# The first block's first layer for the last 768 tokens by Strassen's seven products, with weights combined two batches ahead

## The chip, the cores and the metric

The kernel runs on one core of a Trainium2 chip. The metric is the device time of one execution in microseconds (us), lower is better. Of a core's engines the text names TensorE (PE; its weight loads are PEld), VectorE (DVE), ScalarE (ACT), GpSimd (POOL) and SyncE (SP), which issues the transfers (DMA) here. Line numbers up to the prediction are those of the kernel before.

## What is computed

Three steps in fp32: a block-causal attention (4 batches, 8 heads, 576 tokens of 64 values a head), then a first block of three matrices whose outputs are combined by a maximum, then a second block with four experts:

```python
def _moe_ref(x, w1, w2, w3, w_out):          # x: 2304 x 512, w1..w3: 512 x 768, w_out: 768 x 512
    h = np.maximum(np.maximum(x @ w1, x @ w2), x @ w3)
    return h @ w_out

def _moe2_ref(x, domain_probs, w1, w2):      # w1: 4 x 512 x 1024, w2: 4 x 1024 x 512
    p = domain_probs / (domain_probs.sum(-1, keepdims=True) + 1e-09)
    for e in range(E):
        h = np.maximum(x @ w1[e], 0.0)
        out += p[:, e:e + 1] * (h @ w2[e])
    return out
```

`reference` applies attention, `_moe_ref` and `_moe2_ref` one after the other. The change concerns `x @ w1`, `x @ w2`, `x @ w3` of `_moe_ref` for the last 768 of the 2304 tokens.

## The kernel before

**Precision.** Every matmul of the blocks is made of three: a number is split into a high part and a low part (`f32r` tiles ending in `h` and `l`), and `mm3` (L475, matmul at L480) adds high x high, high x low and low x high in one PSUM tile.

**Attention.** The 16 pairs of heads go one after the other (n = 4 b + d, batch b). A pair's scores (`st`, L181 to L202) are on PE, the row minima (L218) on DVE, the exponentials (L225) on ACT, the sums' reciprocals (L233, L234) on DVE, the division (L251) on POOL; PE transposes the probabilities (`tt`, L279), DVE and ACT copy them out of PSUM (L289), and PE multiplies them with the values (`pv`, L314). Each pair runs its stages beside those of the next one.

**The first block, `moe1(b)` (L505).** Tokens 0 to 511 of a batch (`MAIN`) are one run of 512 columns; the last 64 tokens of each batch (`REST`) are collected in `rest_x`, and all 256 of them are a second run with batch 3. For each of 18 weight tiles (6 blocks `ff` of the hidden width x 3 matrices) a run takes 12 matmuls, over 4 blocks of the inner width with three terms each. The first matrix's result is copied to `mt` or `mr` (L524), the maximum with the others taken by DVE (L526), and POOL splits the hidden values (L528, L529). Then 4 tiles of the output layer take 18 matmuls a run (copied out at L537). Batch 0 splits the weights itself (`Convert`) and stores them to DRAM (`held`); the later batches load them, 512 KB a tile (`moe_weight`, L468).

**What sets the order.** `moe1(b)` is a generator: a unit is up to four matmuls. `Filler.upto` (L540) advances it between the stages of the next batch's attention, in proportion to the pairs done and `LAG` = 9 units behind, so batch b's first block lies under batch b + 1's attention. Batch 3's has no attention to lie under: it runs alone, behind it. Beside it the second block is prepared, with the filler advanced by 8 units between pieces: `combine(0)` (L693) makes the seven sums of token blocks that Strassen's method needs, and `weights_in(0, n)` (L811) loads 512 KB of the second block's weights (`t`, L819), makes their four sums on DVE (`combos`, L790 to L793), splits them (`halves`, ACT L797, DVE L799) and stores 1792 KB (`ka`, L822). The second block already multiplies by Strassen's seven products with 384 columns (L844). SP has one queue of transfers in program order.

## Time and profile before

| | |
|---|---|
| time, median of 3 runs | 1219.99 us (1219.66 to 1220.39) |
| the profiled execution | 1219.63 us, span 1217.7 us |
| PE busy | 1190.4 us, 98% of the span |
| DVE, ACT, POOL busy | 833.7, 466.9, 295.6 us (68, 38, 24%) |
| moved by DMA | 290.67 MB, mean 239 GB/s |

The span is the recorded part of the execution. The page gives busy time by engine and by group of instructions; the chain of waits follows the work that ended last backwards; the windows give busy time by engine in a stretch, the clock that TensorE was granted (PEclk, 1.00 is full) and the share of the DMA engines' time.

### The profile page before, as it was taken

To read this page: it belongs to the slowest core of one execution; us is meant where nothing else is said; L and a number is where in the kernel's file an instruction comes from. 1 tells how busy PE (TensorE), PEld (TensorE's weight loads), DVE (VectorE), ACT (ScalarE), POOL (GpSimd) and SP (SyncE) were. 2 spreads that over 40 slices of the span, in tenths; PEclk is the share of its full clock that TensorE was granted. 3 is DMA by queue.
4 is the path that set the end of the run, shared out by engine and by line. 5 is a ranking of instruction groups with operands and counts; after the bars stand their busy time and mean duration, and the time that the engine had idled before them with its cause. 6 is when DMAs were issued, how large, how long until landed. Compare 5 with 4: busy or idle time off the path is not lost.

```text
span 1217.7 us, 18226 instructions
## 1 busy us (share of the span) xinstructions
PE 1190.4 (98%) x6941; PEld 1065.0 (87%) x6941; DVE 833.7 (68%) x1453; ACT 466.9 (38%) x974; POOL 295.6 (24%) x324
## 2 busy tenths in 40 slices
PE   7889999999999999999999999999999999999998
PEld 4567777778777888898999989999999999999998
DVE  4877874443445541778888895758697887587896
ACT  5976665454335111344434340232232213322222
POOL 2458853433421220433333340000000000000000
PEclk8999999999999999999999999999999999999999
DMA  5836765554423784878888865777887877676664
GB/s 205 274 130 221 247 213 173 164 150 146 139 87 106 272 293 136 302 272 317 319 297 311 303 207 198 282 284 279 344 309 297 322 295 277 233 272 234 250 214 176
DMA packets 82347, 290.67 MB, mean 239 GB/s; under 512 B 8716, under 2 KB 18004, under 8 KB 69204
## 3 DMA queue, kind: packets, MB, share of 16 engines
q1 hardware_dynamic: 82260, 289.51, 67.3%
q8 instruction: 55, 0.90, 0.3%
q14 instruction: 32, 0.26, 0.1%
HBM read 206.34 MB, written 83.14 MB: 238 GB/s over the span
## 4 chain that ended last, share of the span: by engine, by line
PE 80%; DVE 8%; DMA 5%; ACT 4%; issue 2%; POOL 1%; SPq 0%; DVEq 0%; ACTq 0%; POOLq 0%
PE m L844 23%; PE m L480 23%; PE o L1003 16%; PE pv L314 3%; PE tt L279 3%; PE st L181 3%; PE o L926 2%; PE o L930 2%; PE o L929 2%; PE m L1003 2%; DMA part<-in_e_w 2%; ACT p L225 1%; DMA t<-in_e_w 1%; PE st L202 1%; DMA w<-kb 1%
## 5 line engine op out<-in xcount | busy, mean ns | idle before, releaser
L844 PE MATMUL m<-t,w 128*128 128x384 f32 x1152 | 228.4, 336 | 0.0
L1003 PE MATMUL o<-hx,w 128*128 128x384 f32 x1176 | 226.1, 337 | 0.5 <-DMA w<-kb 0.4
L1003 PEld LDWEIGHTS o<-hx,w 128*128 128x128 f32 x1176 | 207.7, 188 | 1.1 <-PE m L844 0.7
L844 PEld LDWEIGHTS m<-t,w 128*128 128x128 f32 x1152 | 203.4, 188 | 2.7 <-DVE tmp L864 0.3
L844 PE MATMUL m<-b,w 128*128 128x384 f32 x864 | 175.5, 336 | 2.1 <-ACT tmp L869 2.1
L844 PEld LDWEIGHTS m<-b,w 128*128 128x128 f32 x864 | 153.1, 188 | 5.6 <-ACT tmp L869 2.4
L480 PE MATMUL m<-xh,wt 128*128 128x512 f32 x352 | 117.4, 396 | 0.0
L225 ACT ACTIVATE p<-st,mn 128x128 f32<-128x128 f32 (+2 forms) x144 | 78.6, 557 | 54.7 <-DVE mn L218 54.7
L864 DVE TENSOR_TENSOR tmp<-m,tmp 128x384 f32<-128x384 f32 x144 | 77.8, 549 | 21.0 <-PE m L844 18.5
L251 POOL TENSOR_SCALAR p<-p,sm 128x128 f32<-128x128 f32 (+4 forms) x108 | 72.0, 683 | 69.1 <-ACT high L119 34.0
L218 DVE TENSOR_REDUCE mn<-st 128x1 f32<-128x128 f32 (+2 forms) x144 | 67.9, 512 | 17.6 <-ACT p L225 9.9
L974 ACT CAST hx<-hq 128x768 fp32r<-128x768 f32 x49 | 40.7, 837 | 97.5 <-PE o L1003 74.2
L480 PEld LDWEIGHTS m<-xh,wt 128*128 128x128 f32 x352 | 65.6, 188 | 12.6 <-ACT arena L537 0.2
L926 PE MATMUL o<-w,hh 128*128 128x512 f32 x192 | 74.8, 392 | 0.5 <-ACT hh L904 0.5
L929 PE MATMUL o<-w,hh 128*128 128x512 f32 x192 | 74.8, 390 | 0.0
L930 PE MATMUL o<-w,hl 128*128 128x512 f32 x192 | 74.7, 391 | 0.0
L279 PE MATMUL tt<-ident,p 128*128 128x128 f32 x400 | 62.7, 286 | 11.2 <-ACT eh L289 6.9
L799 POOL TENSOR_TENSOR w<-part,w 128x512 fp32r<-128x512 f32 x32 | 49.5, 1568 | 92.9 <-ACT w L797 92.9
L279 PEld LDWEIGHTS tt<-ident,p 128*128 128x128 f32 x400 | 48.0, 146 | 25.1 <-ACT eh L289 8.3
L480 PE MATMUL m<-xl,wt 128*128 128x512 f32 x176 | 69.3, 394 | 0.0
L480 PE MATMUL m<-hh,wo 128*128 128x512 f32 x192 | 64.0, 400 | 0.9 <-ACT wo L94 0.9
L799 POOL TENSOR_TENSOR part<-mix,part 128x512 fp32r<-128x512 f32 x32 | 43.8, 1382 | 71.6 <-ACT part L797 65.8
(184 smaller groups left out, 2112.1 us busy)
## 6 DMA issues: line engine op xcount, KB each, us to landing
w<-kb SPq DMA_DIRECT2D x55, 1024.0 KB, 6.0
w<-ka SPq DMA_DIRECT2D x30, 1792.0 KB, 7.9
ka<-w SPq DMA_DIRECT2D x16, 1792.0 KB, 6.7
wt<-held SPq DMA_DIRECT2D x34, 512.0 KB, 4.1
kb<-part SPq DMA_DIRECT2D x16, 1024.0 KB, 6.9
kb<-w SPq DMA_DIRECT2D x16, 768.0 KB, 4.8
arena<-in_w SPq DMA_DIRECT2D x18, 512.0 KB, 4.7
wo<-held SPq DMA_DIRECT2D x12, 768.0 KB, 4.4
```

The lines of the kernel that those rows point to most:

```text
L218: least.append(nc.vector.tensor_reduce(mn[:, m:m + 1], x, axis=AX.X, op=ALU.min))
L225: exps.append(nc.scalar.activation(to, x, ACTF.Exp, bias=mn[:, m:m + 1], scale=-1.0, accum_out=sm[:, m:m + 1],))
L251: normal.append(nc.gpsimd.tensor_scalar(x, x, sm[:, c:c + 1], 1.0, op0=ALU.mult, op1=ALU.mult))
L279: nc.tensor.transpose(tt[:, c:c + P], pt[i][:, k0:k0 + P], ident)
L480: nc.tensor.matmul(out=out_, lhsT=w, rhs=x, start=m == 0, stop=m == n - 1)
L799: eng.tensor_tensor(w[:, a:b, 1], raw[:, a:b], f(w[:, a:b, 0]), op=ALU.subtract)
L844: ins = nc.tensor.matmul(out=m, lhsT=a, rhs=b, start=start and n == 0, stop=stop and n == 3 * KH - 1, skip_group_check=True,)
L864: nc.vector.tensor_tensor(t, x, y, op=ALU.add)
L926: ins = nc.tensor.matmul(out=o, lhsT=hh[:, ts], rhs=wh, start=i == 0, stop=False)
L929: nc.tensor.matmul(out=o, lhsT=hh[:, ts], rhs=wl, start=False, stop=False)
L930: nc.tensor.matmul(out=o, lhsT=hl[:, ts], rhs=wh, start=False, stop=i == G - 1)
L1003: nc.tensor.matmul(out=o, lhsT=a, rhs=b, start=start and m == 0, stop=stop and m == 2, skip_group_check=True,)
```

## The change

Batch 3's first layer and the 256 last tokens are joined to 768 tokens in two halves of 384: tokens 0 to 383 of batch 3, and tokens 384 to 511 of batch 3 with the 256 tokens of `rest_x`. For each matrix n and each two blocks `ff` (9 groups) the 2 x 2 blocks of the weights and of the inputs are multiplied by seven products instead of eight, each product 6 matmuls of 384 columns (`moe1_last`). Three PSUM tiles hold them; partial sums (`u`, `v`, `q1`) are taken out and added by DVE.

The sums of weight blocks that this needs (`t1`, `t2`, `t3`, `b22`) are made by `sums` while batches 1 (groups 0 to 3) and 2 (groups 4 to 8) have the weights in SBUF: DVE adds high and low parts of two tiles (2 x 512 columns), makes four sums (256), ACT casts 1024 columns, DVE subtracts, and 1 MB is stored to DRAM (`summed`); one scratch buffer in `arena` serves all groups. For this, batches 1 and 2 take the tiles of two blocks `ff` in turn. `moe1_last` loads a group's plain parts (`w0` 512 KB, `w1` 256 KB) and its sums (`w2`, 1024 KB, into the tiles `xh` and `xl` in turn).

`rest_x` is one fp32 tile without a low part, and batch 3's inputs are no longer split by `moe1_inputs`; `combine(*ends)` makes the seven sums of inputs behind the attention. The filler's distance in batch 3's attention is 2 x `LAG`. The splitting of batch 3's hidden values is on ACT and DVE instead of POOL. The second block's `weights_in(0, n)` are 14 units apart, and its own `combine` comes behind them.

```diff
+SHARE = 4
...
+    summed = [dram.tile([P, 2, 4, 2 * P], F32, name=f"summed{i}") for i in range(3 * NF // 2)]
...
-    rest_x = [mp.tile([P, KD, B * REST], F32R, name=f"rx{i}", tag=f"rx{i}") for i in range(2)]
+    CT, KH = 384, KD // 2
+    OVER = MAIN - CT
+    NGRP = 3 * NF // 2
+    rest_x = mp.tile([P, KD, OVER + B * REST], F32, name="rx", tag="rx")
...
+            o = OVER + b * REST
+            nc.scalar.copy(rest_x[:, d, o:o + REST], xf[:, MAIN:S])
+            if b == B - 1:
+                nc.scalar.copy(rest_x[:, d, 0:OVER], xf[:, CT:MAIN])
+                continue
+            nc.scalar.copy(xh[:, d], xf[:, 0:MAIN])
+            nc.vector.tensor_tensor(xl[:, d], xf[:, 0:MAIN], f(xh[:, d]), op=ALU.subtract)
...
+    def sums(g, w0, w1):
+        o = 2 * KD * S
+        high, raw = (arena[:, o + i * 8 * P:o + (i + 1) * 8 * P] for i in range(2))
+        for i, w in enumerate((w0, w1)):
+            x = [w[:, j].rearrange("p a f -> p (a f)") for j in range(2)]
+            nc.vector.tensor_tensor(raw[:, i * 4 * P:(i + 1) * 4 * P], f(x[0]), f(x[1]), op=ALU.add)
+        a11, a12, a21, a22 = (raw[:, i * 2 * P:(i + 1) * 2 * P] for i in range(4))
+        nc.vector.tensor_tensor(a22, a21, a22, op=ALU.add)
+        nc.vector.tensor_tensor(a21, a11, a21, op=ALU.subtract)
+        nc.vector.tensor_tensor(a11, a22, a11, op=ALU.subtract)
+        nc.vector.tensor_tensor(a12, a12, a11, op=ALU.subtract)
+        nc.scalar.copy(high.bitcast(F32R), raw)
+        nc.vector.tensor_tensor(raw.bitcast(F32R), raw, high, op=ALU.subtract)
+        nc.sync.dma_start(
+            out=summed[g].rearrange("p x s f -> p (x s f)"), in_=arena[:, o:o + 16 * P]
+        )
...
+        if b:
+            order = [(2 * j + i, n) for j in range(NF // 2) for n in range(3) for i in range(2)]
+        else:
+            order = [(ff, n) for ff in range(NF) for n in range(3)]
...
+            if b and ff % 2:
+                g = 3 * (ff // 2) + n
+                if (g >= SHARE) == (b > 1):
+                    sums(g, last[0], wt)
+            last[0] = wt
...
+    def moe1_last(xc):
+        b = B - 1
...
+                w0 = moe_weight(b, 6 * j + n, at)
+                w1 = moe_weight(b, 6 * j + 3 + n, at + 1, KH)
...
+                nc.sync.dma_start(
+                    out=f(w2).rearrange("p x s f -> p (x s f)"),
+                    in_=summed[3 * j + n].rearrange("p x s f -> p (x s f)"),
+                )
...
+                def product(i, name, start, stop):
+                    first = True
+                    for k in range(KH):
+                        for x, y in ((0, 0), (0, 1), (1, 0)):
+                            nc.tensor.matmul(
+                                out=ms[i], lhsT=side(name, x, k), rhs=xc[name][:, y, k], start=start and first,
+                                stop=stop and (k, x) == (KH - 1, 1), skip_group_check=True,
+                            )
+                            first = False
...
+                def close(key, i, x=None):
+                    if n == 0:
+                        tag = ("mt", "mr")[key[1]]
+                        t = mp.tile([P, (MAIN, CT)[key[1]]], F32, name=tag, tag=tag, bufs=2)[:, 0:CT]
+                        state[key] = t
+                        if x is None:
+                            nc.scalar.copy(t, ms[i])
+                        else:
+                            plus(t, ms[i], x)
+                    else:
+                        t = state[key]
+                        x = ms[i] if x is None else plus(x, ms[i], x)
+                        nc.vector.tensor_tensor(t, x, t, op=ALU.max)
...
+                    for h, l, x in to:
+                        nc.scalar.copy(h, x)
+                        nc.vector.tensor_tensor(l, x, f(h), op=ALU.subtract)
...
+                product(0, "b11", True, False)
+                q1 = temp()
+                nc.scalar.copy(q1, ms[0])
+                yield
+                product(1, "t2", True, False)
+                u = plus(temp(), ms[1], q1)
+                yield
+                product(2, "t1", True, False)
+                v = plus(temp(), ms[2], q1)
+                yield
+                product(0, "b21", False, True)
+                close((0, 0), 0)
+                yield
+                product(1, "t3", False, False)
+                close((1, 1), 1, v)
+                yield
+                product(2, "b22", False, True)
+                close((0, 1), 2, u)
+                yield
+                product(1, "t4", False, True)
+                close((1, 0), 1, q1)
...
-            filler.upto((at - 1) * UNITS - LAG)
+            filler.upto((at - 1) * UNITS - (LAG if b < B - 1 else 2 * LAG))
...
-    following = combine(0)
+    ends = [x for ds in (slice(0, KH), slice(KH, KD)) for x in (x2f[B - 1][:, ds, 0:CT], rest_x[:, ds])]
+    following = combine(*ends)
+    xc = next(following)
+    filler.work.append(moe1_last(xc))
+    for _ in following:
+        filler.upto(filler.done + 1)
+    for n in (2, 3):
+        filler.upto(filler.done + 14)
+        weights_in(0, n)
+    ready = []
+    for n in range(2):
+        filler.upto(filler.done + 14)
+        ready.append(weights_in(0, n))
+    filler.upto(filler.done + 8)
+    following = combine(*blocks(0))
     xc = next(following)
     for _ in following:
-
-        filler.upto(filler.done + 8)
-    weights_in(0, 2)
-    filler.upto(filler.done + 8)
-    weights_in(0, 3)
-    filler.upto(filler.done + 8)
-    ready = [weights_in(0, n) for n in range(2)]
+        filler.upto(filler.done + 4)
```

In the rows of order each line is an instruction or a few alike, with its line in its own kernel. PE at the end of attention, before: transposes of the last pair's probabilities (`tt<-ident,p_...`) and the filler's output layer of batch 2 (`m<-hh,wo`):

```order
L279 MATMUL tt<-ident,p_3903 128x128 x4
L279 MATMUL tt<-ident,p_3782 128x128
L279 MATMUL tt<-ident,p_3780 128x128
L279 MATMUL tt<-ident,p_3782 128x128 x2
L480 MATMUL m<-hl,wo 128x512
L480 MATMUL m<-hh,wo 128x512
L279 MATMUL tt<-ident,p_3911 128x128 x2
L480 MATMUL m<-hh,wo 128x512
L480 MATMUL m<-hl,wo 128x512
L480 MATMUL m<-hh,wo 128x512 x2
L480 MATMUL m<-hl,wo 128x512
L480 MATMUL m<-hh,wo 128x512 x2
```

And in the changed kernel, from the transposes of the last pair to its output product:

```order
L284 MATMUL tt<-ident,p_3889 128x128 x4
L284 MATMUL tt<-ident,p_3755 128x128
L284 MATMUL tt<-ident,p_3753 128x128
L284 MATMUL tt<-ident,p_3755 128x128 x2
L284 MATMUL tt<-ident,p_3897 128x128 x2
L284 MATMUL tt<-ident,p_3902 128x128 x5
L284 MATMUL tt<-ident,p_3891 128x128 x4
L284 MATMUL tt<-ident,p_3763 128x128
L284 MATMUL tt<-ident,p_3761 128x128
L284 MATMUL tt<-ident,p_3763 128x128 x2
L284 MATMUL tt<-ident,p_3899 128x128 x2
L319 MATMUL pv_4149<-eh,vraw 64x384 x2
```

The filler's matmuls (L480, now L487) that stood between the transposes stand behind the last product `pv`.

SP's queue in the middle of the last layer, before: the second block's stores `ka` and loads `t`, and the tiles of the first block (`wt`, `wo` from `held`):

```order
L822 DMA ka_3_4188<-w_4590 128x3584
L819 DMA t<-in_e_w 128x1024
L468 DMA wt<-held_89 128x2x512
L468 DMA wo<-held_90 128x2x512
L468 DMA wo<-held_91 128x2x512
L822 DMA ka_0_4185<-w_4643 128x3584
L819 DMA t<-in_e_w 128x1024
```

And in the changed kernel, where `xh` and `xl` receive the sums:

```order
L958 DMA ka_3_4215<-w_4515 128x3584
L955 DMA t<-in_e_w 128x1024
L603 DMA xh<-summed_103 128x2048
L473 DMA wt<-held_85 128x2x512
L473 DMA wt<-held_88 128x2x256
L603 DMA xl<-summed_104 128x2048
L473 DMA wo<-held_92 128x2x256
L473 DMA wt<-held_89 128x2x512
L958 DMA ka_0_4212<-w_4662 128x3584
```

Between two stores stand two groups' loads, 256 KB and 1 MB pieces among them, where three tiles of 512 KB stood.

DVE under the last pairs of attention, before: minima (L218, with the masks L216), the filler's maxima (L526), the divisors (L233, L234), copies out of PSUM (L289):

```order
L216 MEMSET st 64x64 x4
L218 TENSOR_REDUCE mn<-st 128x1 x4
L526 TENSOR_TENSOR mt<-m,mt 128x512
L233 TENSOR_SCALAR sm<-sm 128x4
L234 RECIPROCAL sm<-sm 128x4
L289 COPY eh<-tt 128x512
L526 TENSOR_TENSOR mt<-m,mt 128x512
L216 MEMSET st 64x64 x2
L218 TENSOR_REDUCE mn<-st 128x1 x2
```

And in the changed kernel, with the sums of a group (L521 to L528) among them:

```order
L528 TENSOR_TENSOR arena<-arena 128x1024
L221 MEMSET st 64x64 x4
L223 TENSOR_REDUCE mn<-st 128x1 x4
L560 TENSOR_TENSOR mt<-m,mt 128x512
L238 TENSOR_SCALAR sm<-sm 128x4
L521 TENSOR_TENSOR arena<-wt 128x512
L239 RECIPROCAL sm<-sm 128x4
L521 TENSOR_TENSOR arena<-wt 128x512
L560 TENSOR_TENSOR mt<-m,mt 128x512
L523 TENSOR_TENSOR arena<-arena 128x256
L524 TENSOR_TENSOR arena<-arena 128x256
L525 TENSOR_TENSOR arena<-arena 128x256
L526 TENSOR_TENSOR arena<-arena 128x256
```

The seven operations of a group (the wide subtract L528 is its last) stand between the minima, divisors and maxima of that stretch.

## Rows read from the trace of the kernel before

**Rows 1.** The page: busy time by engine, and one group of instructions:

```profile
PE 1190.4 (98%) x6941; PEld 1065.0 (87%) x6941; DVE 833.7 (68%) x1453; ACT 466.9 (38%) x974; POOL 295.6 (24%) x324
...
L864 DVE TENSOR_TENSOR tmp<-m,tmp 128x384 f32<-128x384 f32 x144 | 77.8, 549 | 21.0 <-PE m L844 18.5
```

**Rows 2.** Windows of all engines: stretch, length, busy per engine, PEclk, DMA share, GB/s:

```profile
100.00:193.00 93.00, 90.95 (x602) 70.12 (x597) 71.94 (x136) 61.24 (x153) 65.12 (x73) 1.00 0.66 214
193.00:289.00 96.00, 96.00 (x604) 76.05 (x604) 40.57 (x106) 44.25 (x123) 38.02 (x49) 1.00 0.52 158
...
385.00:490.00 105.00, 105.00 (x604) 92.44 (x600) 40.07 (x68) 22.77 (x39) 19.98 (x24) 1.00 0.64 215
```

**Rows 3.** The chain of waits: start, length, what:

```profile
363.41 4.09 PE m L480 x18
...
382.29 2.89 PE pv L314 x40
385.18 104.59 PE m L480 x594
...
511.25 3.13 PE m L844 x18
```

**Rows 4.** The timeline of PE: start, length, line, operation:

```profile
397.69 0.40 PE L480 MATMUL m<-xh,wt 128*128 128x512 f32 x1
...
400.44 1.60 PE L480 MATMUL m<-rx,wt 128*128 128x256 f32 x12
401.87 0.40 PE L480 MATMUL m<-xh,wo 128*128 128x512 f32 x1
```

**Rows 5.** Windows of the filler's matmuls (L480) alone: stretch, length, PE, PEld:

```profile
152.00:185.30 33.30, 22.65 (x91) 16.47 (x91) 1.00 0.67 218
185.30:209.60 24.30, 16.46 (x67) 12.03 (x66) 1.00 0.57 171
```

**Rows 6.** The timeline of the last pair's softmax: start, length, engine:

```profile
369.02 0.75 ACT L225 ACTIVATE p<-st,mn 128x576 f32<-128x576 f32 x1 [2.02 <-DVE mn L218]
...
370.45 3.48 POOL L251 TENSOR_SCALAR p<-p,sm 128x512 f32<-128x512 f32 x5 [3.28 <-DVE sm L234]
...
373.81 0.69 DVE L289 COPY eh<-tt 128x512 f32<-128x512 f32 x1 [1.31 <-PE tt L279]
```

**Rows 7.** Windows of PE alone, around an idle stretch: length, busy, PEclk, DMA:

```profile
52.00:55.40 3.40, 0.94 (x7) 0.97 0.32 86
55.40:58.80 3.40, 3.40 (x15) 0.53 1.00 348
```

**Rows 8.** Groups of DVE by line, 385 to 490 us: busy, mean ns:

```profile
L526 DVE TENSOR_TENSOR mt<-m,mt 128x512 f32<-128x512 f32 x12 | 8.3, 689 | 14.1 <-PE m L480 14.1
L799 DVE TENSOR_TENSOR w<-t,w 128x1024 fp32r<-128x1024 f32 x4 | 6.0, 1510 | 2.1 <-ACT w L797 2.1
...
L799 DVE TENSOR_TENSOR w<-t,w 128x768 fp32r<-128x768 f32 x4 | 4.0, 998 | 0.0
...
L790 DVE TENSOR_TENSOR t<-t 128x256 f32<-128x256 f32 x5 | 2.3, 459 | 15.2 <-DMA t<-in_e_w 15.2
```

**Rows 9.** Windows of highest transfer rate, all engines:

```profile
495.00:515.00 20.00, 19.47 (x101) 17.36 (x100) 16.04 (x26) 8.39 (x17) 9.60 (x8) 1.00 0.99 372
500.00:515.00 15.00, 14.47 (x73) 12.48 (x72) 11.96 (x18) 5.81 (x12) 7.19 (x6) 1.00 1.03 400
```

**Rows 10.** Transfers issued: KB each, us from issue to landing:

```profile
kb<-part SPq DMA_DIRECT2D x16, 1024.0 KB, 6.9
```

**Rows 11.** The timeline of SP: issues of the load t:

```profile
397.22 0.33 SPq L819 DMA_DIRECT2D t<-in_e_w  x1
...
407.99 0.38 SPq L819 DMA_DIRECT2D t<-in_e_w  x1
```

**Rows 12.** The timeline of DVE: first use of t, idle before, releaser:

```profile
401.79 0.42 DVE L790 TENSOR_TENSOR t<-t 128x256 f32<-128x256 f32 x1 [3.40 <-DMA t<-in_e_w]
...
415.64 0.59 DVE L790 TENSOR_TENSOR t<-t 128x256 f32<-128x256 f32 x1 [1.77 <-DMA t<-in_e_w]
```

More of the change, by code (lines that the diff above doesn't have):

```diff
@@ L453, in program, with moe_weight @@
     convert = Convert()
-    def moe_weight(b, n):
+    def moe_weight(b, n, at=0, a0=0):
         if b == 0:
-            wt = convert.weight(n)
-        else:
-            A = tiles[n].shape[1]
-            if b == B - 1 and n == 0:
+            return convert.weight(n)
+        A = tiles[n].shape[1]
+        wide = n >= 3 * NF
+        if b == B - 1 and not wide:
+            if at == 0:
                 taken[0] = 0
-            wide = n >= 3 * NF
-            if b == B - 1 and not wide and n % WT >= 3:
+            if at % WT >= 3:
                 wide = True
                 taken[0] += 1
-            wt = weight_tile(n, wide)
-            nc.sync.dma_start(out=f(wt[:].rearrange("p k a f -> p k (a f)")), in_=held[n][:, :, 0:A * P])
-        return wt[:, 0], wt[:, 1]
+        wt = weight_tile(n, wide)
+        nc.sync.dma_start(
+            out=f(wt[:, :, a0:A].rearrange("p k a f -> p k (a f)")), in_=held[n][:, :, a0 * P:A * P]
+        )
+        return wt
     def split_weights(dst_h, dst_l, raw):
@@ L489, in moe1_inputs @@
     def moe1_inputs(b, ds):
-        if b not in xs:
+        if b < B - 1 and b not in xs:
             xs[b] = (
@@ L531, in moe1, with moe1_out @@
+    def moe1_out(b, runs):
         for d in range(KD):
-            wh, wl = moe_weight(b, 3 * NF + d)
-            for w, _, _, _, hh, hl, to in runs:
+            wt = moe_weight(b, 3 * NF + d)
+            for w, hh, hl, to in runs:
                 m = ps_m.tile([P, 512], F32, name="m", tag="m")[:, 0:w]
-                yield from mm3(m, [(wh[:, ff], wl[:, ff], hh[ff], hl[ff]) for ff in range(NF)])
+                yield from mm3(m, [(wt[:, 0, ff], wt[:, 1, ff], hh[ff], hl[ff]) for ff in range(NF)])
@@ L538, in moe1 @@
                 yield
+    def moe1(b):
+        hidden = [mp.tile([P, NF, MAIN], F32R, name=x, tag=x) for x in ("hh", "hl")]
+        hh, hl = ([x[:, ff] for ff in range(NF)] for x in hidden)
+        xh, xl = xs[b]
+        prev, last = {}, {}
+        if b:
+            order = [(2 * j + i, n) for j in range(NF // 2) for n in range(3) for i in range(2)]
+        else:
+            order = [(ff, n) for ff in range(NF) for n in range(3)]
+        for at, (ff, n) in enumerate(order):
+            wt = moe_weight(b, 3 * ff + n, at)
+            m = ps_m.tile([P, 512], F32, name="m", tag="m")[:, 0:MAIN]
+            yield from mm3(m, [(wt[:, 0, d], wt[:, 1, d], xh[:, d], xl[:, d]) for d in range(KD)])
+            if n == 0:
+                prev[ff] = mp.tile([P, MAIN], F32, name="mt", tag="mt", bufs=2)
+                nc.scalar.copy(prev[ff], m)
+            else:
+                nc.vector.tensor_tensor(prev[ff], m, prev[ff], op=ALU.max)
+            t = prev[ff]
+            if n == 2:
+                nc.gpsimd.tensor_scalar(hh[ff], t, 1.0, 0.0, op0=ALU.mult, op1=ALU.add)
+                nc.gpsimd.tensor_tensor(hl[ff], t, f(hh[ff]), op=ALU.subtract)
+            if b and ff % 2:
[4 more added lines that the diff above has]
+            yield
+        yield from moe1_out(b, [(MAIN, hh, hl, lambda d: x2f[b][:, d, 0:MAIN])])
@@ L613, in program @@
                 ps_m = ps.enter_context(tc.tile_pool(name="ps_m", bufs=2, space=PSUM, reuse_waits="tile"))
-            filler.work.append(moe1(b))
+            if b < B - 1:
+                filler.work.append(moe1(b))
     stage(None)
@@ L1205, in program @@
                 last = ends and it == 1
-                following = combine(1) if last else iter(())
+                following = combine(*blocks(1)) if last else iter(())
                 made = next(following) if last else None
```

87 lines of the change are left out of this document (50 added, 37 removed).

## The prediction, made before the changed kernel had run

> **What bounds the kernel now.** I read the page first: PE is busy 98% of the span, no other engine more than 68% [rows 1]. An average hides stages, so next come windows by stage [rows 2]: PE is full in the stretch from 193 to 289 us (third batch's attention with the second batch's first block under it) and from 385 to 490 us (first block of the fourth batch, alone), and has two idle microseconds in 93 in the stretch from 100 to 193, where VectorE (72 of 93 us) and GpSimd (65 of 93) are busiest. The chain of waits says the same more sharply: after 385.18 us it is one piece of PE work of 104.59 us, 594 matmuls with nothing else in it [rows 3]. So a matmul taken out of there is time, as long as nothing else comes up to PE's pace. VectorE has 40 of 105 us of work there, and the transfers take 0.64 of the DMA engines [rows 2]. The change spends from both.
>
> **What is removed.** PE's rows inside the last layer: a weight tile is twelve matmuls of 512 columns and twelve of 256, from 397.69 to 400.44 and from there to 401.87 us: 2.75 and 1.43 us, or 0.229 and 0.119 each [rows 4]. Eighteen tiles are 18 x 4.18 = 75.2 us. In their place stand nine groups of seven products of six matmuls, 378 of 384 columns. That size is all over the second block: 18 of them took 3.13 us, 0.174 each [rows 3], so 378 take 65.7 us. **PE's work: -9.6 us.** A group is 42 x 0.174 = 7.3 us. The output layer (24.9 us) keeps its matmuls.
>
> **What is moved: the end of attention.** The filler's lag in the last batch goes from 9 to 18 units: 36 matmuls (8.2 us) move from under the last attention to behind it, where they cover the making of the combined inputs. PE's total is the same, but the order shows no filler left between the two last output products. Count from T, the end of the last scores (363.41 us [rows 3]). Before, T to 385.18 is 21.8 us, and is filled: 58 filler matmuls of 0.229 (13.3), two output products of 2.89 (5.8) [rows 3], 25 transposes (2.7). After, only 3 filler matmuls stand there, so PE has 0.7 + 2.9 + 2.7 = 6.3 us of work before the last output product. Its inputs take longer: the five exponentials run on ScalarE in order, two of 512, two of 256 and one of 576 columns, 0.75 for the widest [rows 6], with the steps that read their sums 4.1 us, one waits for a copy of pair 14's output, and two small VectorE steps follow: first normalisation at T + 5.0 to T + 5.9. GpSimd's five normalisations are 3.48 us [rows 6], so the last ends at T + 8.5 to T + 9.4. Transposes behind it, the copy out of PSUM (0.69 [rows 6]) and the handovers between four engines are 1.9 to 2.6 us. The last product can start at about T + 11.1, 4.8 us after PE has run out. **+4.8 (3.5 to 6).** Before, this chain was just as long and lay under the filler.
>
> An idle stretch can cost once more. PE was busy 0.94 us in the 3.4 us after 52, and the next 3.4 us, fully busy, ran at a granted clock of 0.53, the lower of the two levels (1.2 of 2.4 GHz) [rows 7]. The same length at half clock here is 1.7 us of lost work; the transposes in the gap keep PE partly busy. **+0.7 (0 to 1.7).**
>
> **What is added under batches 1 and 2: the sums.** Each of nine groups gives VectorE two 512-wide adds (0.69), four 256-wide (0.42 to 0.46), and a 1024-wide subtract (1.51) [rows 8]: 1.4 + 1.7 + 1.5, about 4.6 us, 41 us in all; ScalarE gets one cast each. Four groups fall in the stretch 193 to 289, where VectorE has 40.6 of 96 us [rows 2], so 59 of 96; five in the next, 63 of 96 if that is like it. On average there is room. But VectorE works in order, and one scratch buffer serves all: a group's first add waits until the previous 1 MB has been stored, for which the nearest row gives 6.9 us [rows 10], and the next scores' masks and maxima are queued behind that add (the order shows them). PE then waits for the probabilities of a pair. The nearest row for a busy VectorE is the first batch's conversion: the pair from 152 to 185.3 has 91 filler matmuls, so 33.3 - 20.8 = 12.5 us beside them, the pair after it 24.3 - 67 x 0.229 = 9.0 [rows 5]: 3.5 us in one pair of the worst stage. Here eight pairs carry sums, each milder. No excess at all is as possible as two bad pairs. **+2.5 (0 to 5).**
>
> **What is added in the last layer: transfers.** Before, a tile needs 512 KB. Now a group needs w0 512, w1 256 and its sums 1024 KB, and four groups' time also sees the second block's weights pass (a 512 KB load, a 1792 KB store), as before. Two groups and one of those are 5888 KB = 6.03 MB in 14.6 us of PE. The most that the trace shows over 15 us is 400 GB/s, over 20 us 372 [rows 9]: 15.1 or 16.2 us. That alone is 0.5 to 1.6 us for each of four. The queue makes it worse. SP issues in order and a load behind a store lands late: t, issued at 397.22 with nothing in front, could be used at 401.79; issued at 407.99 just behind a ka store it was used at 415.64, 7.6 against 4.6 us [rows 11, 12]. And a group's sums can be fetched only when the group two before has used its own in its sixth product, and are wanted in its second: 1/7 + 1 + 1/7 groups later, 9.4 us. Where a store falls in that window, store, t, sums, w0 and w1 are 1.835 + 0.524 + 1.049 + 0.524 + 0.262 = 4.19 MB: 10.5 us at 400 GB/s, 11.3 at 372, so 1.1 to 1.9 us late. I take 1.5, four times. **+6 (2 from the bare rate, 12 if each is late by those 3 us).**
>
> The Trainium skill ("DMA: Bandwidth & Descriptors", section "Where 436 GB/s comes from") says that transfers between HBM and SBUF are bound by the HBM side at about 358 GB/s. By that the 4.19 MB would take 11.7 us, 2.3 late, and the term would be 9 instead of 6, the sum 1228. This trace's 400 GB/s over 15 us speaks against it as a ceiling, so it enters no number here.
>
> **VectorE in the last layer.** Per group two PSUM adds, then one to six more of 384 columns (0.55 [rows 1]), and in each third group the low parts: about 2.8, 5.0 and 7.4 us, 45 in nine groups; with four times 4.3 us for the second block's weights (four adds and the subtracts of 1.51 and 1.00 [rows 8]) 62 of 65.7 us. A full engine that works in order lets PE wait now and then. PE has six PSUM buffers and runs three ahead. **+1 (0 to 4).** The second combination of inputs and the last of those weights lie beside the output layer's 24.9 us: 0, and up to 2 if VectorE is late.
>
> **Sum** against the profiled execution, 1219.63 us (span 1217.7 and 1.9 around it; the median of the runs is 0.4 us more, so no correction): 1219.6 - 9.6 + 4.8 + 0.7 + 2.5 + 6 + 1 = **1225.0**. Its own range is 1221 to 1229.
>
> **Rivals.**
> *The transfers are hidden.* If the stores don't hold back the loads, two groups' loads are 3584 KB, 9.2 us at 400 GB/s against 14.6 of PE, and the last layer runs at PE's pace: 1225 - 6 = 1219, no difference. For: two groups are loaded ahead, under the moved filler. Against: the loads of t [rows 11, 12]. It decides where sums land within 9.4 us of the release of their buffer. Chance 0.25.
> *The other side: VectorE and the gap are covered too.* If besides that the sums find their place in VectorE's free 55 of 96 us and the half clock doesn't come, 1219.6 - 9.6 + 4.8 = 1214.8. It decides where no store of sums is awaited by an add with scores behind it. For: the full PE between 193 and 289, although VectorE is 42% busy. Chance 0.17.
> *VectorE and the transfers lock step.* weights_in's subtracts wait for their load, the PSUM adds queue behind them, PE for those, and the next sums for PE. With the upper ends in that layer (12 and 4): 1225 + 6 + 3 = 1234, and less where they overlap: 1233. For: 62 of 66 us. Chance 0.13.
> *It doesn't do what it says:* PE's order has the 378 matmuls, so no.
>
> **How the numbers follow.** The forecast has 0.45. A measurement of this kernel tells about 0.2% (2.4 us) from no change, so faster is below 1217.5, slower above 1222.4. Faster: nearly all of the second rival and a little of the first, 0.20. Same: most of the first and the low end of the forecast, 0.24. Slower: the rest, 0.56. The range that should hold 8 in 10 goes from 1215 (half of the second rival outside) to 1232 (most of the third outside).
>
> **What would show it.** Right: in PE's windows 66 us of matmuls in the last layer in a stretch some 6 to 8 longer, with waits there for summed or held; an idle PE of 4 to 5 us before the last output product, released by the copies out of the transposes, and a granted clock under 1.00 just behind; pairs of batches 2 and 3 longer than 9.0 us plus their filler. Wrong: a last layer of 66 us without waits (the first rival), pairs unchanged as well (the second), or waits for VectorE rather than for transfers. A filler that still covers the last softmax would overturn the term that I hold to be the surest.

## The result, and the profile after

The changed kernel takes 1236.26 us (median of 4 executions, 1234.49 to 1238.21) against 1219.97 us (4 executions, 1219.66 to 1220.39): a ratio of 1.0134, 95% interval 1.0116 to 1.0151. It is slower by 16 us where 5 were forecast, and lies above the range. Line numbers are now those of the changed kernel (scores' minima L223, normalisation L256, transposes L284, PV L319, three-term matmuls L487, the sums L521 to L528, the seven products L617). The profiled execution is the longest of the four, 1238.21 us with a span of 1236.4.

The page first (busy time by engine), as in [rows 1]:

```profile
PE 1191.0 (96%) x6887; PEld 1068.6 (86%) x6887; DVE 903.2 (73%) x1570; ACT 484.9 (39%) x1008; POOL 282.9 (23%) x300
```

PE's busy time is where it was (1190.4 before), although 9.6 us of work are gone. A lower clock has filled part of the place: the same work takes 1183.9 us in e10 below, and where the granted clock was 0.50 a matmul of 512 columns took 0.425 us instead of 0.229. VectorE has 70 us more. Windows by stage, all engines (stretch, length, busy per engine with counts, PEclk, DMA share, GB/s), as in [rows 2]:

```profile
193.00:289.00 96.00, 94.11 (x573) 74.35 (x573) 51.96 (x120) 42.98 (x116) 38.15 (x47) 0.98 0.62 201
289.00:385.00 96.00, 90.45 (x592) 69.98 (x590) 59.41 (x131) 41.98 (x116) 36.02 (x44) 1.00 0.55 186
```

```profile
405.00:490.00 85.00, 80.15 (x451) 76.17 (x449) 64.51 (x123) 26.60 (x49) 0.00 (x0) 1.00 0.76 288
490.00:510.30 20.30, 15.68 (x75) 13.38 (x75) 2.12 (x6) 2.31 (x6) 0.00 (x0) 0.83 0.47 152
```

PE was full from 193 to 490 us before. Now 2 and 5.5 us are missing in the two attention stretches with sums, 5 in the last layer, and 4.6 in the output layer. The granted clock was 0.83 in the output layer and 0.98 in the first of the attention stretches.

Adding up needs the same marks in both traces. Attention ends at 385.1 us before and 392.0 after, with 36 matmuls (8.2 us) fewer inside it: +15.1. From there to the end of the first block it was 104.4 us and is 118.0; the work is 103.0 (54 matmuls of 0.229 that now stand there, 36 of them moved, 378 of 0.174, and the output layer's 24.9), so +15.0 over the work. The second block is 1.8 us shorter (726.4 against 728.2). In sum 15.1 + 15.0 - 9.6 - 1.8 = 18.7, the difference of the spans.

**The first 15 us, in attention.** 0.8 us lie ahead of 100 us, where executions differ by more than that (the output product that starts at 99.3 us here starts at 97.5 in e14 and at 100.8 in e5, with the same operations up to there). 3.3 are the gap at the end. The other 11 are in the pairs, of which three stand out. Windows of the filler (L487) alone, one pair each (length, PE with count), as in [rows 5]:

```profile
185.90:217.50 31.60, 21.09 (x80) 15.62 (x79) 0.95 0.64 209
...
318.50:352.70 34.20, 23.46 (x97) 17.59 (x96) 1.00 0.60 201
352.70:379.80 27.10, 17.26 (x66) 11.78 (x66) 1.00 0.56 209
```

Taking the filler off at 0.229 each leaves 13.3, 12.0 and 12.0 us; in the kernel before the same pairs leave 9.0 to 9.3. The chain of waits (start, length, what) says what released them:

```profile
190.12 4.84 DMA summed<-arena
202.55 7.37 PE m L487 x24
...
327.79 4.68 DMA summed<-arena
342.73 4.68 DMA summed<-arena
353.22 4.62 DMA summed<-arena
364.39 5.16 DMA summed<-arena
...
412.26 7.67 DMA t<-in_e_w
...
462.69 9.35 DMA xh<-summed
...
494.73 15.53 PE m L487 x72
```

Five times it is the store of the sums. Around the first, the timelines of VectorE, then ScalarE, then PE (start, length, operation, in brackets the idle time before it and its releaser):

```profile
195.06 1.29 DVE L521 TENSOR_TENSOR arena<-wu 128x512 f32<-128x512 f32 x2 [3.80 <-DMA summed<-arena]
196.36 0.18 DVE L221 MEMSET st<- 64x64 f32 x2
...
197.30 1.39 DVE L223 TENSOR_REDUCE mn<-st 128x1 f32<-128x128 f32 x4
```

```profile
198.73 0.37 ACT L230 ACTIVATE p<-st,mn 128x128 f32<-128x128 f32 x1 [4.11 <-DVE mn L223]
...
201.88 0.61 ACT L558 COPY mt<-m 128x512 f32<-128x512 f32 x1
```

```profile
202.55 0.50 PE L487 MATMUL m<-xh,wu 128*128 128x512 f32 x1 [1.84 <-ACT mt L558]
```

The add of the next group (L521) waits 3.8 us until `summed` has been stored; the masks (L221) and minima (L223) of the next scores stand behind it; ScalarE's exponentials wait 4.1 us for those, its copy of a finished PSUM tile (L558) stands behind the exponentials, and PE waits for that tile. The wait on PE (1.8 us) is shorter than the one on VectorE and comes 7 us later. It costs a second time: the 24 matmuls behind it took 7.37 us by the chain, where 24 of 0.229 are 5.5, because the granted clock fell to its lower level:

```profile
203.40:206.80 3.40, 3.40 (x10) 0.54 0.35 100
```

So 1.8 us of waiting and 1.9 of lower clock are most of the 4.3 us by which this pair grew. The other two pairs kept a clock of 1.00 and grew by 3.0 each.

In the gap at the end of attention PE waits three times, 2.8 us in all, for the last pair's probabilities and for the copies behind their transposes. On VectorE the last group's sums stand ahead of that pair's minima:

```profile
384.17 1.56 PE L284 MATMUL tt<-ident,p 128*128 128x128 f32 x10 [1.37 <-POOL p L256]
...
389.06 0.87 PE L319 MATMUL pv<-eh,vraw 128*64 128x384 f32 x4 [0.73 <-ACT eh L294]
```

```profile
375.22 1.23 DVE L528 TENSOR_TENSOR arena<-arena 128x1024 fp32r<-128x1024 f32 x1 [0.56 <-ACT arena L527]
377.20 1.29 DVE L223 TENSOR_REDUCE mn<-st 128x1 f32<-128x512 f32 x2
```

**The second 15 us, behind attention.** PE's timeline shows the waits of the last layer one by one; the two largest before the output layer, and the largest of all in it:

```profile
443.43 1.32 PE L617 MATMUL m<-t,xh 128*128 128x384 f32 x6 [1.42 <-DVE arena L589]
...
472.08 2.35 PE L617 MATMUL m<-t,xh 128*128 128x384 f32 x12 [1.18 <-DMA xh<-summed]
...
494.73 0.79 PE L487 MATMUL m<-hh,wo 128*128 128x512 f32 x1 [4.62 <-DMA wo<-held]
```

The waits in the first layer are 4.8 us in all: 2.5 for VectorE's adds (L589), 1.6 for `summed` and 0.7 for ScalarE's copy of `q1` (L652; ScalarE takes it out of PSUM, not VectorE). The first layer takes 7.5 us more than its work; the rest isn't in single waits that the timeline shows. In the output layer PE stands still for 4.62 us, waiting for a weight tile; behind that, windows of PE (length, busy, PEclk):

```profile
494.70:498.10 3.40, 3.37 (x8) 0.50 0.74 268
498.10:501.50 3.40, 3.40 (x11) 0.63 0.00 0
```

The clock is at the lower level (0.50 of 2.4 GHz) for 3.4 us and partly in the next; the 72 matmuls after the wait took 15.5 us where 36 of 512 and 36 of 256 columns are 12.5. So this one wait costs 4.6 + 2.9 = 7.5 us.

### The profile page after: what moved, and what is told of

It reads as the page before. It is cut to its first block, busy times and chain, and to the rows that moved or that the text cites. A ratio compares the mean times of both kernels' runs of the same rounds, so it can differ in the third digit from the quotient of the medians.

```text
span 1236.4 us, 18275 instructions
## 1 busy us (share of the span) xinstructions
PE 1191.0 (96%) x6887; PEld 1068.6 (86%) x6887; DVE 903.2 (73%) x1570; ACT 484.9 (39%) x1008; POOL 282.9 (23%) x300
## 4 chain that ended last, share of the span: by engine, by line
PE 72%; DVE 10%; DMA 9%; ACT 5%; issue 2%; POOL 1%; SPq 0%; DVEq 0%; ACTq 0%; POOLq 0%
PE m L980 24%; PE o L1139 17%; PE m L487 13%; PE m L617 3%; PE tt L284 2%; PE pv L319 2%; PE st L186 2%; PE o L1062 2%; ACT p L230 2%; PE o L1066 2%; PE o L1065 2%; DMA summed<-arena 2%; PE m L1139 2%; DMA t<-in_e_w 2%; DMA part<-in_e_w 2%
## 5 line engine op out<-in xcount | busy, mean ns | idle before, releaser
L256 POOL TENSOR_SCALAR p<-p,sm 128x128 f32<-128x128 f32 (+4 forms) x108 | 78.7, 743 | 105.7 <-ACT high L124 51.5
L487 PE MATMUL m<-xh,wt 128*128 128x512 f32 x256 | 85.7, 400 | 0.0
L223 DVE TENSOR_REDUCE mn<-st 128x1 f32<-128x128 f32 (+2 forms) x144 | 68.1, 512 | 16.5 <-ACT p L230 7.3
L284 PE MATMUL tt<-ident,p 128*128 128x128 f32 x400 | 62.0, 286 | 16.1 <-ACT eh L294 6.6
L284 PEld LDWEIGHTS tt<-ident,p 128*128 128x128 f32 x400 | 47.2, 145 | 30.5 <-ACT eh L294 8.3
L487 PE MATMUL m<-hh,wo 128*128 128x512 f32 x192 | 66.2, 411 | 6.6 <-DMA wo<-held 5.0
L1110 ACT CAST hx<-part 128x768 fp32r<-128x768 f32 x28 | 23.3, 836 | 91.4 <-PE o L1139 69.4
L1111 DVE TENSOR_TENSOR hx<-hq,hx 128x768 fp32r<-128x768 f32 x49 | 46.7, 955 | 16.0 <-ACT hx L1110 15.7
```

The costliest lines, as they stand in the source:

```text
L223: least.append(nc.vector.tensor_reduce(mn[:, m:m + 1], x, axis=AX.X, op=ALU.min))
L256: normal.append(nc.gpsimd.tensor_scalar(x, x, sm[:, c:c + 1], 1.0, op0=ALU.mult, op1=ALU.mult))
L284: nc.tensor.transpose(tt[:, c:c + P], pt[i][:, k0:k0 + P], ident)
L487: nc.tensor.matmul(out=out_, lhsT=w, rhs=x, start=m == 0, stop=m == n - 1)
```

## The experiments

Each is the changed kernel with the edit shown, unless another is named. Its expectation is quoted first. The times are medians, compared with the kernel before in the same set of runs (1219.6 to 1220.3 us).

### e1, e6: is it the store of the sums or VectorE's work?

```diff
-                if (g >= SHARE) == (b > 1):
+                if g % 2 == (b > 1):          # e1: even groups in batch 1
+                if (g + 1) % 2 == (b > 1):    # e6: odd groups in batch 1
```

> The same nine groups of sums, but even groups in batch 1 and odd ones in batch 2, so that a group has two weight pairs' time (some 17 us instead of 8.5) before the next wants the one scratch buffer. Theory A (the 11 us by which pairs 8 to 14 grew beside their filler are the wait for the store of the scratch buffer, with the score minima queued behind it on VectorE): 7 to 11 us less than the changed kernel's 1236.3, so 1225 to 1229. Rival (it is VectorE's 41 us of additional work, or the 9 MB of stores, which stay): 1235 to 1238.

Measured: 1235.25 us (1232.80 to 1236.86), so by the total the theory fell. The trace says otherwise for half of it. In batch 2 the pairs' excess went from 6 us to 0.4, with the same VectorE work for each group. In batch 1 there were two new waits, of 2.44 and 4.65 us. SP's timeline and PE's, with the clock behind it:

```profile
278.43 0.33 SPq L529 DMA_DIRECT2D summed<-arena  x1
278.85 19.72 SPq L473 DMA_DIRECT2D wo<-held  x4
```

```profile
285.66 0.80 PE L487 MATMUL m<-hh,wo 128*128 128x512 f32 x1 [4.65 <-DMA wo<-held]
```

```profile
285.70:289.10 3.40, 3.40 (x8) 0.50 0.22 92
```

The weights of batch 1's output layer (`wo`) were issued just behind the last group's store, which SP held until VectorE had finished that group. The last group was an even one. That gave the next form of the edit:

> Sums of odd groups in batch 1 and of even ones in batch 2. After the run e1_spread theory A is: a group costs nothing where the store has twice the time (batch 2 there: 0.4 us in place of 6.1), and what was left in batch 1 is the first group, which met the last conversion, and the last one, whose store stood ahead of the output layer's weights in SP's queue. With the odd ones in batch 1 neither is there: pairs 8 to 11 grow by under 3 us, and 1225 to 1229 in all. Rival (in batch 1 the sums cost 6 to 13 us wherever they lie): 1233 to 1238.

Measured: 1225.82 us (1223.11 to 1227.85, ratio 1.0044, interval 1.0026 to 1.0061), 10.4 us less than the changed kernel, with every group's operations and bytes unchanged. Windows of PE in the two attention stretches:

```profile
193.00:289.00 96.00, 94.02 (x580) 1.00 0.64 210
289.00:385.00 96.00, 95.13 (x651) 1.00 0.52 175
```

Between the profiled executions (11.0 us) the gain lies in three places. The pairs' excess falls by 6.4 us; by the pairs some 5 us are left of the 11. The gap at the end of attention falls by 2.6 of its 3.3 us, although the filler is as far behind as in the changed kernel: PE waits only once, 0.73 us, before the last output product, the sums are done on VectorE by 355.4 us, and 19 filler matmuls stand between the last scores and the product of the pair before, where the changed kernel has 3.

```profile
379.41 0.87 PE L319 MATMUL pv<-eh,vraw 128*64 128x384 f32 x4 [0.73 <-ACT eh L294]
```

About 1 us is behind attention, and the rest is ahead of the sums. What the sums cost is thus for the larger part the distance between a group's store and the next use of its buffer, and what stands behind both in the two queues. The 5 us that are left may be the 41 us of VectorE or the 9 MB; no run here takes these away, so that is open.

### e2, e5: why was the output layer's weight tile late?

```diff
+        if b == B - 1 and n >= 3 * NF:        # e2: the four loads, the tails' stores and the
+            tc.keep_in_program_order(ins)     #     load of (1, 0) in weights_in, in program order
...
-                nc.tensor.matmul(out=out_, lhsT=w, rhs=x, start=m == 0, stop=m == n - 1)
+                ins = nc.tensor.matmul(...)   # e5: the output layer of the last batch
+                if keep:
+                    tc.keep_in_program_order(ins)
```

> The output layer's four weight loads of the last batch, the saving of the tails and the first load of expert 1 stay in the order of the program on SP. Theory B (the 4.6 us stall in the output layer is SP's queue: the last two weight tiles stand behind a load that waits for its scratch tile until 486 us; 2.9 us more are the lower clock behind the stall): 6 to 8 us less, 1228 to 1231. Rival (the tiles are late because the transfers themselves are slow there, or their buffers come free late): 1235 to 1238, the stall still there.

Measured: 1245.89 us (1242.89 to 1248.36). Theory B in that form fell. Nothing but the four loads stood in that part of SP's queue, and PE's wait was where it had been:

```profile
462.66 27.08 SPq L473 DMA_DIRECT2D wo<-held  x4
```

```profile
493.61 0.80 PE L489 MATMUL m<-hh,wo 128*128 128x512 f32 x1 [4.23 <-DMA wo<-held]
```

Four loads issued over 27 us means that the last two waited for a buffer. The 10 us more are a side effect of the edit, which also moved the load for expert 1 far back: the second block took 736.0 us instead of 726.4. PE's order had the cause: the first two output tiles are worked on in turns, so both buffers of `wo` are held until 489 us.

> The changed kernel with one difference: the output layer's matmuls of the last batch stay in the order of the program on PE (tile 0 for 512, then for 256 columns, then tile 1). After the run e2_queue theory B is: the first two output tiles are worked on in turns, both of the two weight buffers come free together at 489 us, and the last two tiles' loads can't begin before. Then the stall of 4.6 us and the 2.9 us of lower clock behind it go: 1229 to 1232. Rival (SP's queue, held by the load for expert 1 until 486 us, is enough by itself): the loads come at 486 to 487 and 1 to 3 us go, 1233 to 1235.

Measured: 1234.56 us (1228.73 to 1236.46), 1.7 less with 8 us between executions; in the traces the stretch behind attention is 3 us shorter (115.0 against 118.0). The wait for weights is gone, but two others have come, and they too are followed by a low clock (0.67 from 484.8 to 490). PE's timeline, then VectorE's at the same time:

```profile
483.07 0.49 PE L487 MATMUL m<-hh,wo 128*128 128x512 f32 x1 [0.73 <-ACT hh L648]
484.82 0.60 PE L487 MATMUL m<-hl,wo 128*128 128x512 f32 x1 [1.25 <-DVE hl L649]
```

```profile
482.60 0.95 DVE L806 TENSOR_TENSOR t<-t,t 128x768 fp32r<-128x768 f32 x1
...
485.14 0.56 DVE L649 TENSOR_TENSOR hl<-mt,hh 128x384 fp32r<-128x384 f32 x1
```

PE waits for the last hidden values (high part L648, low part L649). On VectorE they stand between the 768-wide subtracts (L806) of the second block's combination of inputs. They stood there in the changed kernel too, where PE had first-layer products left for that time. So both theories of the expectation lacked one cause.

### e9, e10, e11: the causes together

```diff
+                        if j == NF // 2 - 1:              # e10: the last hidden values' low parts,
+                            tc.keep_in_program_order(ins)
-    filler.upto(filler.done + 8)
-    following = combine(*blocks(0))
+    filler.upto(filler.done + 22)                         #      then the combination
+    following = combine(*blocks(0), keep=True)
...
-                        ins = nc.vector.tensor_tensor(l, x, f(h), op=ALU.subtract)
+                        ins = nc.gpsimd.tensor_tensor(l, x, f(h), op=ALU.subtract)    # e11
```

> The edits of e6 (odd groups' sums in batch 1, even ones in batch 2) and of e5 (output layer of the last batch in program order on PE) together. If the two causes are separate, their differences add: -10.4 and -1.7 from 1236.3, so 1224. If the output layer's stall only changes its place (e5: the wait for weights became 2 us of waits for hidden values and 2 us of lower clock), it stays within 1 us of e6's 1225.8.

Measured: 1223.29 us (1222.53 to 1224.21), 2.5 less than e6: the differences add. What is left of the output layer's wait is for the last hidden values:

```profile
472.28 0.74 PE L487 MATMUL m<-hh,wo 128*128 128x512 f32 x1 [2.17 <-ACT hh L648]
```

> e9 with the second block's combination of inputs moved behind the low parts of the last hidden values on VectorE (and with it the load for expert 1 behind the third output tile's weights). Theory W (what was left of the output layer's 7.5 us is VectorE's queue: the second combination, 10 us of VectorE, stood ahead of the last hidden values): 3 to 5 us less than e9, about 1220. Rival (the second combination is then late for the second block, which waits as long): as e9 or slower, with the wait at the second block's first products.

Measured: 1219.54 us (1217.01 to 1220.95, ratio to before 0.9993, interval 0.9981 to 1.0005). 3.8 us less than e9, as theory W had it, and the second block is no longer than before (725.9). PE's waits of the output layer have shrunk to one:

```profile
469.44 0.50 PE L487 MATMUL m<-hh,wo 128*128 128x512 f32 x1 [0.24 <-ACT hh L648]
```

From the changed kernel to this one it is 16.7 us without a change of the arithmetic. Of the versions that compute the same result it is the fastest here, and no faster than the kernel before.

> e10 with the low parts of the last batch's hidden values on GpSimd (idle there) instead of VectorE, 7 us of VectorE in the last layer. Theory V (VectorE, in order and 62 of 66 us busy, makes the first layer's waits): 2 to 3 us less than e10. Rival (GpSimd's slower subtracts come late for the output layer, and VectorE slows beside them): no gain, or up to 3 us slower.

Measured: 1225.67 us (1221.56 to 1228.01), 6 us slower than e10: the rival, by twice what it allowed. PE's timeline:

```profile
451.02 2.27 PE L619 MATMUL m<-t,xh 128*128 128x384 f32 x6 [3.24 <-DVE arena L591]
...
476.52 0.50 PE L487 MATMUL m<-hl,wo 128*128 128x512 f32 x1 [2.11 <-POOL hl L649]
```

The second wait is plain: GpSimd's low part comes late. The first, 3.2 us for an add of VectorE (0.88 in e10 at the same place), has its reason in the timelines just ahead of it: VectorE in e10, then VectorE and GpSimd in e11:

```profile
443.44 0.42 DVE L933 TENSOR_TENSOR t<-t 128x256 f32<-128x256 f32 x1
```

```profile
444.19 0.96 DVE L933 TENSOR_TENSOR t<-t 128x256 f32<-128x256 f32 x1
...
445.68 0.96 DVE L934 TENSOR_TENSOR t<-t 128x256 f32<-128x256 f32 x1
```

```profile
443.81 1.06 POOL L649 TENSOR_TENSOR wu<-mr,wu 128x256 fp32r<-128x256 f32 x1
```

In e10, where GpSimd is idle in this layer, VectorE's 256-wide operations take 0.41 to 0.43 us; beside GpSimd's subtracts four of them here took 0.41 to 0.96. The 2.27 us for six matmuls behind the wait (1.2 elsewhere) are the lower clock again (0.51 granted from 451.0 to 454.4).

### e4, e7, e12, e15: the filler's distance

```diff
-            filler.upto((at - 1) * UNITS - (LAG if b < B - 1 else 2 * LAG))
+            filler.upto((at - 1) * UNITS - LAG)          # e7; e12: the same in e10; e15: 14 in e10
```

> The kernel before with one part of the change: the filler 18 units behind instead of 9 in the last batch. Theory D (the last softmax is no longer covered): the trace of the changed kernel has 3.3 us more there beside the filler, so 1223 to 1224; the prediction's own terms give 4.8 + 0.7, 1225.5. Rival (the gap came from late sums in the last pairs, not from the filler): within 1 us of 1220.

Measured: the kernel before with 2 x `LAG` in the last batch takes 1224.85 us (1222.19 to 1226.72), +5.2 by the medians (ratio 1.0035, interval 1.0018 to 1.0051). Its trace has the gap, at an unbroken clock of 1.00:

```profile
374.15 1.86 PE L279 MATMUL tt<-ident,p 128*128 128x128 f32 x15 [1.22 <-POOL p L251]
376.74 0.87 PE L314 MATMUL pv<-eh,vraw 128*64 128x384 f32 x4 [0.73 <-ACT eh L289]
```

By the marks, 2.7 us are the gap, 0.4 more follow before the first block ends, and 1.3 are in the second block, which this edit doesn't touch; those can't be told from the difference between two executions. So the distance alone makes the gap in the kernel before. There the split of batch 3's inputs (L503, 2.3 us in the chain) still stands on VectorE ahead of the last minima; the changed kernel doesn't have it, and in e6 the same distance left 0.73 us. In the changed kernel the gap takes the late sums too.

> The changed kernel with the filler 9 units behind in the last batch, as before. Theory D: the gap at the end of attention (3.3 us) closes, and 18 matmuls (4.1 us) still cover the first of the combined inputs: 1232 to 1234. Rival (the 18 units are needed behind attention to cover the seven combinations): 1236 to 1240, with a wait for them before the first product.

Measured: 1238.09 us (1237.39 to 1240.24). The gap closed (2.6 of its 3.3 us), and the total grew by 1.8: the rival. PE's waits tell where it went:

```profile
415.17 1.39 PE L617 MATMUL m<-t,wt 128*128 128x384 f32 x6 [1.82 <-DVE mr L589]
...
483.79 0.73 PE L487 MATMUL m<-hh,wo 128*128 128x512 f32 x2 [3.45 <-ACT hh L646]
```

With 36 matmuls less behind attention (18 instead of 54), the first products catch up with VectorE, where the combined inputs and a weight tile of the second block stand ahead of their adds (L589), and the last hidden values (L646) come late.

> e10 with the filler 9 units behind in the last batch. Theory D: the gap of 3 us at the end of attention closes; with 18 matmuls less behind attention the first products wait for their inputs and sums (e7: 1.8 us at the start of the layer, and the last group's values came late): between 2 us less and 2 us more than e10. Under 1219.9 it would beat the kernel before.

> e10 with the filler 14 units behind in the last batch (9 before, 18 in the change). e12 (9 units) was 4.8 us slower than e10, because the layer's first inputs and the last hidden values came late; the gap at 18 units is 2 to 3 us. If both are steep only at their ends, 14 is 1 to 2 us faster than e10, 1217.5 to 1218.5; if the waits in the layer grow evenly with what is taken away, 1 to 2 us slower.

Measured: 1224.36 us (1222.16 to 1226.09) with 9 units and 1219.97 us (1217.05 to 1224.51) with 14, against 1219.54 with 18. The expectations took the gap of the changed kernel, 2 to 3 us, but in e10 PE waits only 0.73 us before the last output product, so there was little to win. With 9 units that wait is gone, and the stretch behind attention is 3.6 us longer for its work; 14 can't be told from 18 by these totals.

### e3, e8, e13, e14: transfers or VectorE in the last layer?

```diff
-                    out=f(w2).rearrange(...), in_=summed[3 * j + n].rearrange(...),
+                    out=f(w2)[:, 0].rearrange(...), in_=summed[3 * j + n][:, 0].rearrange(...),    # e3, e13
...
-        halves(w, raw, [(nc.vector, 0, 4), (nc.vector, 4, 7)])
+                    nc.scalar.copy(w[:, x:y, i], raw[:, x:y])    # e8, e14: both halves, expert 0
```

> In the last layer only the high halves of the combined weights are loaded (512 instead of 1024 KB a group) and used in place of the low halves too; the matmuls' count and everything on VectorE is as before. Theory C (the first layer's 6.7 us beyond its matmuls are transfers): 4 to 6 us less, 1230 to 1232. Rival (it is VectorE, 62 of 66 us busy there): within 1.5 us of 1236.3.

> The second block's first four weight tiles get their low parts by a ScalarE copy instead of VectorE's subtract, which takes some 9 us of VectorE out of the last layer and puts 7.5 us onto ScalarE (31% busy there). The low parts are then the whole values, so the second block's result for that expert is another one. Theory V (the first layer's 5 us of waits are VectorE's): the waits for it go, 2 to 4 us less, 1232 to 1234. Rival (they follow from transfers and from the release of PSUM by ScalarE): within 1.5 us of 1236.3, or more.

Measured: 1233.88 us (1231.16 to 1237.49) and 1234.01 us (1232.94 to 1236.83): 2.4 and 2.2 less: the first between its theory and its rival, the second at the lower end of its theory. The stretch from the end of attention to the end of the first block is 114.1 and 114.6 us in their traces, against 118.0.

> e10 with half of the combined weights' bytes loaded in the last layer (high halves only, also used as low ones). If transfers hold the first layer's remaining waits: 3 to 4 us less than e10's 1219.5, so 1215.5 to 1216.5. If it is VectorE: within 1.5 us of e10.

> e10 with the low parts of the second block's first four weight tiles made by ScalarE copies (whole values instead of low parts), some 9 us of VectorE less in the last layer. If VectorE holds the remaining waits: 2 to 3.5 us less than e10's 1219.5, so 1216 to 1217.5. If transfers do: within 1.5 us of e10.

Measured: 1218.15 us (1216.16 to 1219.99) and 1218.74 us (1215.19 to 1221.30), 1.4 and 0.8 less than e10 with 4 to 6 us between executions. Of the profiled ones the stretch is 107.5 and 108.8 us against 111.2 in e10, so 3.7 and 2.4 us less, while attention, which is the same program in all three, ended at 382.4, 378.9 and 380.5 us. By the totals alone neither is shown; by the stretch, in one execution each, both count, the transfers somewhat more. All four compute another result (the high half of each combined weight used twice, or whole values as low parts), so they price a wait and are no versions to keep.

## Why the prediction was wrong

- **PE's work, -9.6 us: right.** The stretch behind attention is longer than its work by what the waits and the clock largely explain, with 0.174 us for each of the 378 products.
- **The sums under batches 1 and 2, +2.5 (0 to 5): the step that failed, 11 us.** The mechanism was named as it is (a single buffer, the add behind a store, the minima behind the add, PE behind the probabilities), but its price was taken from one pair of the first batch's conversion and averaged with zero, and the lower clock behind PE's wait (1.9 of the 11 us) wasn't in it. It could have been worked out. The two weight tiles of a group are 24 filler matmuls, 5.5 us of PE, some 8 to 9 us with the attention beside them; a turn of the buffer is the seven operations (4.6), the cast (1) and the store (4.7 to 6.9), so 10 to 12.5; the stores of the last five groups were issued 10.5 to 14.9 us apart. A loop that is slower than the work it hangs on isn't averaged out by VectorE's idle time: it falls behind at each group, until PE waits. e6 gave the loop twice the time and took back 10.4 us, of which 6.4 are in the pairs and 2.6 in the gap at the end of attention. The 5 us left in the pairs stay open.
- **The output layer, 0 (up to 2): failed, 7.5 us.** I weighed the length of what lies beside it and not the order: which buffers its loads need and when these come free, and that the second combination stands on VectorE ahead of the last hidden values. Both were to be seen in the changed kernel's order on PE and VectorE. e5 removed the one, e10 the other; with both, and the sums respaced, the excess is gone.
- **The last layer's transfers and VectorE, +7: right in size, 7.5, but not as split.** I had 6 for transfers and 1 for VectorE. PE's waits are 1.6 us for `summed` and 2.5 for VectorE's adds, and taking away half of the sums' bytes or 9 us of VectorE shortened the stretch by about as much (3.9 and 3.4 us in e3 and e8, 3.7 and 2.4 in e13 and e14). That the total fits is in part luck.
- **The gap at the end of attention, +4.8: right in kind, 3.3, but not the filler's alone.** The chain is as long as forecast: the last output product starts 10.8 us after the last scores, 11.1 were forecast. But that only 3 filler matmuls were left to cover it goes with the late sums: in e6, with the same distance and the sums spaced, 22 stand there and PE waits 0.73 us. That the filler's moved matmuls were needed behind attention (e7, e12) I had said, without a price for it.
- **The lower clock, +0.7: at the wrong place, and too small.** The gap left the clock at 1.00; the wait of 1.8 us in the first pair with sums cost 1.9 more, and the standstill of 4.6 us in the output layer 2.9. Both are contained in the 11 and 7.5 us above.
- The second block is 1.8 us shorter, which I had at 0. It takes 725.8 to 726.8 us in every traced run of the changed kernel's kind but e2, and 728.1 and 729.3 in the kernel before and in e4, so it isn't chance; what shortens it was not tried. 0.8 us at the start and the difference between the profiled 1238.2 and the median of 1236.3 are differences between executions.

The Trainium skill's rule ("DMA: Bandwidth & Descriptors", section "Where 436 GB/s comes from") that transfers between HBM and SBUF are bound at about 358 GB/s was set aside, and the trace bears that out. Windows of PE in the last layer (the last two columns are the DMA share and GB/s):

```profile
425.00:445.00 20.00, 18.16 (x102) 1.00 1.02 411
```

With 411 GB/s over 20 us the queue had more than the rule allows, and was full (1.02).

The second rival had the size of the other side's gain right (-9.6 and the gap), and nothing of what was in its way. The third rival, VectorE and transfers in lock step, came nearest with 1233, but for a reason that accounts for the smaller part.

## What to carry to other kernels

When side work is hung on a loop through one buffer, compare a full turn of that buffer (operations, cast, store, wait) with the time that the host loop takes for one turn: if it is longer, the delay adds up however idle the engines are, and spacing the turns brings back much of it without making the work cheaper (a second buffer was not tried here). An engine that works in order passes a wait on to all that stands behind it, so read on each engine's order what is queued behind every new wait, also where two pieces of moved work end up together. And cover that is moved from one place to another is paid for where it is taken away.

## What the runs showed of the hardware that was not expected

Of three idle stretches of PE in the same program, the one in three pieces at the end of attention (2.8 us in all, transposes between) left the granted clock at 1.00. The one of 1.84 us in one piece was followed by 3.4 us at 0.54, and the one of 4.62 us by 3.4 us at 0.50 and 3.4 at 0.63; with the clock they cost 3.7 and 7.5 us. In e1 a wait of 4.65 us was followed by 0.50 in the same way, while in e11 one of 2.11 us left the clock at 1.00; so the length of a wait alone doesn't tell, and these runs don't settle what does. GpSimd's subtracts made some of VectorE's operations beside them up to twice as long (e11: 0.96 for 0.42 us). And the same program's executions spread by 0.3% and more: the kernel before took 1216.4 to 1224.4 us in the later sets, so differences of 1 us between variants are not shown here.
